# A written order for VectorE and GpSimd in a two-level Strassen feed-forward, on one core

## The chip, the cores and the metric

The kernel runs on one core of a Trainium2 chip. The metric is the device time in microseconds (us). Before the change it is 1205.03 us, the median of two runs (1204.66 and 1205.40). The profile is one further execution, with a span of 1208.1 us from its first to its last instruction.

## The reference

Batches of 576 tokens and 512 columns go through an attention whose key and query softmaxes are taken apart (so that keys times values comes first), then through a Fourier mixing layer, a layer norm and a feed-forward with residual:

```python
# B, H, S, DH = 8, 8, 576, 64;  D = 512;  FF = 2048
q_s = softmax(q, axis=-1);  k_s = softmax(k, axis=2)
x = q_s @ (k_s^T @ v)                    # per head; heads are put side by side: (8, 576, 512)
u = x + real(fft(fft(x, axis=1), axis=2))
un = (u - mean(u)) / sqrt(var(u) + 1e-6)
out = u + maximum(un @ w_ch1, 0) @ w_ch2  # w_ch1 (512, 2048), w_ch2 (2048, 512), all float32
```

## The kernel before

Tokens are taken in nine groups of 512 (own rows of eight batches, and one group of rows that all batches leave over). The program is written for a tile framework with a scheduler: the order of the source gives priorities, and the scheduler fixes, when the program is built, in which order each engine takes its instructions. Semaphores follow from the data.

The feed-forward of group 0 is plain. In groups in places 1 to 8 both matrix products are done with Strassen's seven products for a 2 x 2 split; the additions on the small side are made on the chip, those on the weights once and kept in DRAM. A product is numbered 1 to 7 and taken in `ORDER`; sums are made while PSUM is evicted:

```python
ORDER = (1, 6, 5, 7, 2, 4, 3)
# strassen(): one job = seven products into three PSUM banks ba, bb, bc
ends = {1: copy ba to s1 (ScalarE),
        6: u2 = bb + s1 (VectorE),
        7: u3 = bb + s1 (VectorE), out[2, 2](bc, u3),
        2: out[1, 1](ba), 4: out[2, 1](bb, s1), 3: out[1, 2](bc, u2)}
at = {1: "ba", 2: "ba", 6: "bb", 7: "bb", 4: "bb", 5: "bc", 3: "bc"}
```

The first layer (`up`, matmuls at L986) has four such jobs, called blocks here. `out` applies ReLU: for (1, 1) on ScalarE alone, for the others a VectorE addition (L997) and a ScalarE ReLU (L998). When a block is complete, GpSimd makes the four combinations of the hidden activations that the second layer's products need:

```python
def a_side(self, at, to, e1, e2):          # L377 to L380, both engines are GpSimd here
    e1.tensor_tensor(out=to(4), in0=at(2), in1=at(3), op=ALU.add)
    e1.tensor_tensor(out=to(2), in0=at(0), in1=at(2), op=ALU.subtract)
    e2.tensor_tensor(out=to(5), in0=to(4), in1=at(0), op=ALU.subtract)
    e2.tensor_tensor(out=to(6), in0=at(1), in1=to(5), op=ALU.subtract)
```

In the six groups in places 2 to 7 (`deep`), the second layer (`deep_down`, matmuls at L1091) is two-level: each of its seven products m is itself cut into seven sub-products n, 49 in all, of four 128x128 matmuls each. The products come in units that share banks. Before the sub-products of a unit, the same four additions are made on the quarters of its hidden activations (L1048), half on VectorE and half on GpSimd, while the unit before runs. Product 1 needs only the (1, 1) part of the first layer's result:

```python
UNITS = ((1,), (2, 4), (7, 6), (5, 3))
def a_steps(unit):
    for m in unit:
        to = own(m)
        for o, x, y, e, op in ((4, 2, 3, V, ALU.add), (2, 0, 2, V, ALU.subtract), (5, 4, 0, G, ALU.subtract),
                               (6, 1, 5, G, ALU.subtract)):
            steps.append(lambda ...: e.tensor_tensor(out=to(o), in0=to(x), in1=to(y), op=op))     # L1048
...
steps = a_steps(UNITS[0])
for i, unit in enumerate(UNITS):
    ahead = a_steps(UNITS[i + 1]) if i + 1 < len(UNITS) else []
    steps += mixed(unit_steps(unit), ahead) + after[unit]     # after: results added to x by GpSimd (L1054, L1057)
```

The weights of the second level are made in the group in place 1: `deepen` splits each of the seven combined parts of w2 into seven and stores them in DRAM.

Beside the feed-forward of a group runs the front of the next batch: the attention beside the first layer, the Fourier mix and the norm beside the second. The Fourier transform is folded by symmetry before its matmuls:

```python
def tokens_folded():   # L728: eo[i] = x[i % 2, 0] +- x[i % 2, 1], i < 2 on GpSimd, else VectorE
def columns_folded():  # L734: eo[i][1:256] +-= mirrored half, the same engines
def by_frequency():    # L743: sums of pairs of eo, i < 2 on GpSimd, else VectorE
def columns_again():   # L749, L750: eight VectorE additions on 128 columns
folds = [tokens_folded, columns_folded, by_frequency, folded]   # folded: columns_again, then the next keys' loads
return folds + [lambda: None] * (b > 1) + [lambda k=k: block(k) for k in (2, 3, 0, 1, 4)]
...
jobs, down = blk.up(order, unT), blk.down(g, order, unT)
merged(flat(jobs), one)                       # one: attention of the next batch
merged(down, two + norm(next group))          # two: folds, transform blocks, mixes
```

Of the kernel before, what the change touches and what calls it, by code (L numbers as in the profile page):

```python
# [40 lines left out]
F32 = mybir.dt.float32  # L41
# [37 lines left out]
UNITS = ((1,), (2, 4), (7, 6), (5, 3))  # L79
DEEP = [(m, n) for unit in UNITS for n in ORDER for m in unit]  # L80
PAIRS = [(j + NP // 2, j) for j in range(NP // 2)]
# [46 lines left out]
class _Block:  # L128
    def __init__(self, ctx, tc, q, kT, v, w1, w2, ft, cd, out):
# [46 lines left out]
        for at in range(1, B + 1):  # L176
            self.base[at] = len(self.plan)
            self.plan += [self.w1s[p][:].rearrange("p a n -> p (a n)") for pair in PAIRS for p in pair]
            if self.deep(at):
                for i in range(0, len(DEEP), 4):  # L180
                    self.plan.append(self.w2d[:, i:min(i + 4, len(DEEP)), :].rearrange("p a n -> p (a n)"))
            else:
                self.plan += [self.w2s[WB_AT[m]].rearrange("p a n -> p (a n)") for m in ORDER]
# [298 lines left out]

    def second_keys(self):
# [83 lines left out]
    def k_exp(self, it):  # L567
        nc, V = self.nc, self.nc.vector
        k = self.live[it][0]
        m = self.small.tile([P, 1], F32, tag="km", name="km", bufs=3)  # L570
        V.reduce_max(m[:], k, axis=AX.X, negate=True)
        rec = self.small.tile([P, 1], F32, tag="krec", name="krec", bufs=3)
        nc.scalar.activation(k, k, ACT.Exp, bias=m[:, 0:1], accum_out=rec[:, 0:1])
        V.tensor_scalar(out=rec[:], in0=rec[:], scalar1=ATT_EPS, scalar2=None, op0=ALU.add)
        V.reciprocal(rec[:], rec[:])
        self.live[it].append(rec)
# [15 lines left out]
    def k_times_v(self, it):  # L592
        nc, (_, b, r) = self.nc, it
        _, v, rec, ks = self.live.pop(it)
        pk = self.acc((P, P))
        for c in range(NC):
            nc.tensor.matmul(pk, lhsT=ks[:, c, :], rhs=v[:, c, :], start=(c == 0), stop=(c == NC - 1))  # L597
        for h in range(2):
            s = slice(64 * h, 64 * h + 64)
            to = self.kvr[b % 2][s, r, s]  # L600
            if b == 1:

                nc.scalar.mul(to, pk[s, s], rec[s, 0:1])
            else:
                nc.vector.tensor_scalar(out=to, in0=pk[s, s], scalar1=rec[s, 0:1], scalar2=None, op0=ALU.mult)
# [22 lines left out]
    def q_exp(self, it):  # L628
        nc, V = self.nc, self.nc.vector
        q = self.live[it][0]  # L630
        heads = q.rearrange("p (h d) -> p h d", h=H)
        spread = lambda t: t[:].unsqueeze(2).to_broadcast([P, H, DH])
        m = self.small.tile([P, H], F32, tag="qm", name="qm", bufs=3)
        V.reduce_max(m[:], heads, axis=AX.X, negate=True)  # L634
        for h in range(H):
            nc.scalar.activation(heads[:, h, :], heads[:, h, :], ACT.Exp, bias=m[:, h:h + 1])  # L636
        rec = self.small.tile([P, H], F32, tag="qrec", name="qrec", bufs=4)
# [3 lines left out]
        if it[:2] == ("q", 0) and it[2] == it[3]:  # L641


            self.live[it].append(spread(rec))
            return
# [21 lines left out]
    def t_fold(self, it):  # L667
# [4 lines left out]
        for e, op, i in ((G, ALU.add, 0), (V, ALU.subtract, 2)):  # L672
            e.tensor_tensor(out=T[:, :, i, 1:NT], in0=q[:, :, 1:NT], in1=q[:, :, W - 1:W - NT:-1], op=op)
            e.tensor_tensor(out=T[:, :, 1 + i, 1:NT - 1], in0=q[:, :, Q - 1:Q - NT + 1:-1],
                            in1=q[:, :, Q + 1:Q + NT - 1], op=op)
        n = NT - 1
# [5 lines left out]
    def q_times_kv(self, it):  # L682
# [3 lines left out]
        for r in range(NR):  # L686
            nc.tensor.matmul(px[:, r * P:(r + 1) * P], lhsT=qT[:, r, :], rhs=self.kvr[b % 2][:, r, :], start=True,  # L687
                             stop=True)
        x = self.xpart(b, c, u)
# [6 lines left out]
    def t_times_kv(self, b):  # L696
# [9 lines left out]
        nc.scalar.copy(self.xshared(b // 2)[part], px[W:])  # L706
        V.scalar_tensor_tensor(out=g[:, 1:HD], in0=g[:, D - 1:HD:-1], scalar=self.sign[:, 0:1], in1=g[:, 1:HD],
# [3 lines left out]
        self.live["g", b] = g  # L711
# [3 lines left out]
    def transform(self, b):  # L715
# [36 lines left out]
        def folded():  # L752
            columns_again()
# [39 lines left out]

        folds = [tokens_folded, columns_folded, by_frequency, folded] if b else [at_first]
# [140 lines left out]
    def strassen(self, product, out, early=lambda *a: None):  # L935
# [30 lines left out]
        for m in ORDER:  # L966
# [4 lines left out]
            steps.append(begin + parts + end)  # L971
        return steps

    def up(self, at, unT):
# [4 lines left out]
        for j in range(NP // 2):  # L979
# [24 lines left out]
            steps.append([s for m in job for s in m] + [lambda n=base + 2 * j + i: self.used(n) for i in range(2)])  # L1004
# [21 lines left out]
    def deep_down(self, g, at, unT):  # L1026

        nc, V, G = self.nc, self.nc.vector, self.nc.gpsimd
        base = self.base[at] + NP
        un = lambda i: unT[:, i].rearrange("p k n -> p (k n)").rearrange("p (f n) -> p f n", n=P)  # L1030
        dead = lambda m: [self.hblock(A_AT[m], a, b) for a, b in ((0, 1), (1, 0), (1, 1))]
        temps = {1: [self.gap(i) for i in range(3)], 4: [un(i) for i in range(3)], 2: [un(i) for i in range(3, 6)],
                 6: dead(1), 7: [self.gap(i) for i in range(3)], 5: dead(4), 3: dead(2)}
        result = {m: self.hblock(A_AT[m], 0, 0) for m in A_AT}
        tile = lambda m: result[m].rearrange("p (c e) n -> p c e n", c=2)

# [5 lines left out]
        def a_steps(unit):  # L1042
            steps = []
            for m in unit:
                to = own(m)
                for o, x, y, e, op in ((4, 2, 3, V, ALU.add), (2, 0, 2, V, ALU.subtract), (5, 4, 0, G, ALU.subtract),
                                       (6, 1, 5, G, ALU.subtract)):
                    steps.append(lambda to=to, o=o, x=x, y=y, e=e, op=op: e.tensor_tensor(out=to(o), in0=to(x), in1=to(y),  # L1048
                                                                                          op=op))
            return steps  # L1050
# [8 lines left out]
        def store(u):  # L1059
            for c in range(2):  # L1060
                self.store(g, c, u, self.xpart(g, c, u))

        after = {(1,): [lambda: into(0, 0, 1)],
                 (2, 4): [lambda: into(1, 0, 4), lambda: into(0, 0, 2)],
                 (7, 6): [lambda: sums(6, 1), lambda: into(0, 1, 6), lambda: sums(7, 6), lambda: into(1, 0, 7),
                          lambda: into(1, 1, 7)],
                 (5, 3): [lambda: into(1, 1, 5), lambda: store(1), lambda: into(0, 1, 5), lambda: into(0, 1, 3),
                          lambda: store(0)]}
        place = {1: "ba", 2: "ba", 6: "bb", 7: "bb", 4: "bb", 5: "bc", 3: "bc"}

        def unit_steps(unit):
            k, box = len(unit), {}

            def bank(n):
                box[n] = self.ps.tile([P, 2, P], F32, tag=n, name=n)

            def temp(n):
                box[n] = self.work.tile([P, 2, P], F32, tag=n, name=n, bufs=1)
                return box[n][:, 0:k]

            def product(n):
                def run(i):
                    m, to = unit[i], own(unit[i])
                    q = DEEP.index((m, n))
                    w = self.stream[base + q // 4]
                    first = n in (1, 6, 5)
                    if first and i == 0:
                        bank(place[n])
                    for f in range(4):
                        r = q % 4 * 4 + f  # L1090
                        nc.tensor.matmul(box[place[n]][:, i, :], lhsT=to(A_AT[n])[:, f, :],  # L1091
                                         rhs=w[:, r // 2, r % 2 * P:r % 2 * P + P], start=first and i == 0 and f == 0,
                                         stop=f == 3, skip_group_check=True)
                    if q % 4 == 3 or q == len(DEEP) - 1:
                        self.used(base + q // 4)
                return [lambda i=i: run(i) for i in range(k)]

            def plus(out, n, t):
                V.tensor_tensor(out=out, in0=box[n][:, 0:k], in1=t[:, 0:k], op=ALU.add)  # L1099

            def block(j, n, t=None):
                slots = [A_AT[m] for m in unit]
                out = self.hpairs(j)[:, slots[0]:slots[-1] + 1:max(slots[-1] - slots[0], 1), 0:P]
                if t is None:
                    nc.scalar.copy(out, box[n][:, 0:k])
                else:
                    plus(out, n, box[t])

            ends = {1: lambda: nc.scalar.copy(temp("s1"), box["ba"][:, 0:k]),  # L1109
                    6: lambda: plus(temp("u2"), "bb", box["s1"]),  # L1110
                    7: lambda: (plus(temp("u3"), "bb", box["s1"]), block(3, "bc", "u3")),
                    2: lambda: block(0, "ba"), 4: lambda: block(2, "bb", "s1"), 3: lambda: block(1, "bc", "u2")}
            steps = []
            for n in ORDER:
                steps += product(n) + ([ends[n]] if n in ends else [])
            return steps

        steps = a_steps(UNITS[0])
        for i, unit in enumerate(UNITS):
            ahead = a_steps(UNITS[i + 1]) if i + 1 < len(UNITS) else []  # L1120
            steps += mixed(unit_steps(unit), ahead) + after[unit]
        return steps

    def down(self, g, at, unT):
# [6 lines left out]
        def product(m, bank, first, final):  # L1131
# [6 lines left out]
            def run(i, q):  # L1138
                w = self.stream[n]
                if at == 1 and (i, q) == (order[0], 0):  # L1140
# [38 lines left out]
        return [s for m in steps for s in m]  # L1179
# [22 lines left out]
def kernel(ctx: ExitStack, tc: tile.TileContext, q, kT, v, w1, w2, ft,  # L1202
# [56 lines left out]

    groups = [*range(B - 1), B, B - 1]  # L1260
    for order, g in enumerate(groups):
        loads = [] if g == 0 else None
        one, two = front(order + 1, loads) if order + 1 < B else (blk.later, [])
# [46 lines left out]
        jobs, down = blk.up(order, unT), blk.down(g, order, unT)  # L1310

# [56 lines left out]
```

## Time and profile before

The spans are those of the profiled execution. TensorE is PE, its weight loads PEld, VectorE is DVE, ScalarE is ACT, GpSimd is POOL.

| what | value |
|---|---|
| device time | 1205.03 us |
| POOL idle before L377 of a block, waiting for ACT's ReLU | 251.5 us in 26 waits |
| PE matmuls of the first layer (L986), bank bb | 188.2 us, 768 records |
| PE matmuls of the second level (L1091), bank bb | 124.3 us, 912 records |
| additions L1048 on DVE | 76.0 us, 72 of them, 1075 ns each |
| additions L1048 on POOL | 91.7 us, 60 of them, 1537 ns each |
| DMA | 239.85 MB, mean 199 GB/s |

A timeline row gives start, length, engine, source line, operation, what it writes and reads, and how many instructions were merged; in brackets stands how long the engine was idle before it and what released it. A row of waits gives who waited for whom, the total in us, how often, and the longest. A row of busy time by stage gives the stretch, then for each engine its busy us and the number of instructions, and last the granted clock of TensorE (1.00 is full), the busy share of the DMA engines and GB/s. In the row of 40 slices each digit is the busy share in tenths.

### The profile page before, as it was taken

Reading aid. Unit: us, or ns where it says so; the run is one execution under the profiler, and the core shown is the slowest. Engines: PE = TensorE matmul, PEld = TensorE weight load, DVE = VectorE, ACT = ScalarE, POOL = GpSimd, SP = SyncE. Lnnn points to the kernel's source line nnn. Section 1 sums busy time; section 2 is a strip of 40 time slices with the busy share of each in tenths; the row PEclk is TensorE's granted clock in tenths of the full one; section 3 lists DMA queues with packets and bytes.
Section 4 is the critical chain, followed back from the end, with each engine's and each line's share of the span. In section 5 each row is a group of like instructions: output and inputs, shape, how many; then the busy total and the mean of one; then the engine's idle time right before and its main releaser. Section 6 shows DMA issues by size and latency. Waiting matters only on the chain.

```text
span 1208.1 us, 17183 instructions
## 1 busy us (share of the span) xinstructions
PE 1088.4 (90%) x6384; PEld 938.5 (78%) x6384; DVE 685.7 (57%) x1303; ACT 416.9 (35%) x1015; POOL 550.0 (46%) x449
## 2 busy tenths in 40 slices
PE   5799899988899699987999699969999799889998
PEld 4644457877788698877989698859988798789886
DVE  6784874477436884487445963586635743352211
ACT  6694424351216323361325232431334052101200
POOL 1075650355323654357333854276434834663420
PEclk9999999988999899998999899989999799989999
DMA  9475775576966356554565457635654456465541
GB/s 300 150 244 184 256 254 182 182 257 204 309 206 223 127 205 218 200 189 172 207 216 180 171 187 227 207 126 210 233 183 149 150 201 210 162 216 206 211 175 56
DMA packets 117507, 239.85 MB, mean 199 GB/s; under 512 B 24480, under 2 KB 77984, under 8 KB 106416
## 3 DMA queue, kind: packets, MB, share of 16 engines
q1 hardware_dynamic: 115624, 237.70, 57.1%
q10 hardware_dynamic: 1800, 1.05, 0.3%
q8 instruction: 51, 0.84, 0.3%
q14 instruction: 32, 0.26, 0.1%
HBM read 201.76 MB, written 41.16 MB: 201 GB/s over the span
## 4 chain that ended last, share of the span: by engine, by line
PE 66%; DVE 11%; POOL 7%; issue 2%; ACT 2%; DMA 1%; SPq 0%; POOLq 0%; DVEq 0%; ACTq 0%
PE bb L986 13%; PE bb L1091 9%; PE bc L986 8%; PE ba L986 8%; PE bc L1091 6%; PE ba L1091 5%; PE acc L597 2%; PE bc L1143 2%; PE acc L687 2%; DVE big L1048 2%; PE bb L1143 2%; POOL unT L1048 2%; PE bc L925 1%; POOL eo L728 1%; PE tr L886 1%
## 5 line engine op out<-in xcount | busy, mean ns | idle before, releaser
L986 PE MATMUL bb<-unT,big 128*128 128x256 f32 x768 | 188.2, 382 | 4.6 <-DVE unT L386 4.6
L1091 PE MATMUL bb<-big 128*128 128x128 f32 x912 | 124.3, 290 | 53.0 <-DVE big L1048 30.2
L986 PEld LDWEIGHTS bb<-unT,big 128*128 128x128 f32 x768 | 143.7, 191 | 26.2 <-DVE unT L386 7.4
L377 POOL TENSOR_TENSOR big<-big 128x512 f32<-128x512 f32 (+1 forms) x38 | 47.4, 1246 | 252.3 <-ACT big L998 251.5
L1091 PEld LDWEIGHTS bb<-big 128*128 128x128 f32 x912 | 116.4, 204 | 56.7 <-DVE big L1048 31.1
L998 ACT ACTIVATE big<-big 128x512 f32<-128x512 f32 x96 | 60.1, 629 | 211.2 <-DVE big L997 211.1
L986 PE MATMUL bc<-unT,big 128*128 128x256 f32 x512 | 125.6, 381 | 2.2 <-DVE unT L384 2.2
L986 PE MATMUL ba<-unT,big 128*128 128x256 f32 x512 | 122.7, 379 | 0.2 <-ACT unT L890 0.2
L1048 POOL TENSOR_TENSOR big<-big 128x512 f32<-128x512 f32 x60 | 91.7, 1537 | 38.0 <-DVE big L1048 34.2
L986 PEld LDWEIGHTS bc<-unT,big 128*128 128x128 f32 x512 | 95.3, 191 | 15.9 <-PE ba L986 4.0
L986 PEld LDWEIGHTS ba<-unT,big 128*128 128x128 f32 x512 | 95.3, 190 | 12.3 <-ACT unT L890 0.5
L1091 PE MATMUL ba<-big 128*128 128x128 f32 x672 | 90.4, 286 | 1.3 <-ACT s L1109 1.3
L1054 POOL TENSOR_TENSOR x<-x,big 128x512 f32<-128x512 f32 x45 | 65.4, 1469 | 55.8 <-DVE big L1099 39.7
L1091 PEld LDWEIGHTS ba<-big 128*128 128x128 f32 x672 | 86.2, 202 | 3.4 <-ACT s L1109 1.9
L1048 DVE TENSOR_TENSOR big<-big 128x512 f32<-128x512 f32 x72 | 76.0, 1075 | 13.8 <-POOL big L379 6.7
L958 DVE TENSOR_TENSOR u<-bb,s 128x512 f32<-128x512 f32 x34 | 23.5, 691 | 86.4 <-PE bb L986 65.7
L1091 PE MATMUL bc<-big 128*128 128x128 f32 x480 | 63.1, 284 | 7.0 <-DVE big L997 7.0
L1091 PEld LDWEIGHTS bc<-big 128*128 128x128 f32 x480 | 59.7, 200 | 7.5 <-DVE big L997 7.5
L636 ACT ACTIVATE q<-q,qm 128x64 f32<-128x64 f32 x240 | 61.7, 339 | 7.8 <-DVE qm L634 7.8
L997 DVE TENSOR_TENSOR big<-bc,u 128x512 f32<-128x512 f32 x64 | 44.1, 689 | 25.5 <-PE bc L986 24.1
L1099 DVE TENSOR_TENSOR u<-bb,s 128x256 f32<-128x256 f32 (+1 forms) x48 | 18.4, 384 | 69.2 <-PE bb L1091 68.8
L954 DVE TENSOR_TENSOR u<-bb,s 128x512 f32<-128x512 f32 x34 | 23.4, 690 | 58.6 <-PE bb L986 44.0
(276 smaller groups left out, 2112.0 us busy)
## 6 DMA issues: line engine op xcount, KB each, us to landing
big<-w2d SPq DMA_DIRECT2D x72, 1024.0 KB
big<-w1s SPq DMA_DIRECT2D x64, 896.0 KB
big<-w2s SPq DMA_DIRECT2D x14, 1024.0 KB
w2d<-big SPq DMA_DIRECT2D x49, 256.0 KB
big<-in_w_dram SPq DMA_DIRECT2D x21, 512.0 KB
q<-in_q_dram SPq DMA_DIRECT2D x27, 256.0 KB
k<-in_kT_dram SPq DMA_DIRECT2D x24, 288.0 KB
v<-in_v_dram SPq DMA_DIRECT2D x24, 256.0 KB
```

What stands on the lines that cost most here:

```text
L377: e1.tensor_tensor(out=to(4), in0=at(2), in1=at(3), op=ALU.add)
L597: nc.tensor.matmul(pk, lhsT=ks[:, c, :], rhs=v[:, c, :], start=(c == 0), stop=(c == NC - 1))
L636: nc.scalar.activation(heads[:, h, :], heads[:, h, :], ACT.Exp, bias=m[:, h:h + 1])
L687: nc.tensor.matmul(px[:, r * P:(r + 1) * P], lhsT=qT[:, r, :], rhs=self.kvr[b % 2][:, r, :], start=True, stop=True)
L958: V.tensor_tensor(out=temp("u3"), in0=box["bb"][:], in1=box["s1"][:], op=ALU.add)
L986: nc.tensor.matmul(bank()[:, i, :], lhsT=w[:, WA_AT[m], k * P:(k + 1) * P], rhs=unT[:, B_AT[m], k, :], start=first and i == 0 and k == 0, ...
L997: V.tensor_tensor(out=hp(i), in0=bank[:], in1=u[:], op=ALU.add)
L998: nc.scalar.activation(hp(i), hp(i), ACT.Relu)
L1048: steps.append(lambda to=to, o=o, x=x, y=y, e=e, op=op: e.tensor_tensor(out=to(o), in0=to(x), in1=to(y), op=op))
L1054: G.tensor_tensor(out=x, in0=x, in1=tile(m), op=ALU.add)
L1091: nc.tensor.matmul(box[place[n]][:, i, :], lhsT=to(A_AT[n])[:, f, :], rhs=w[:, r // 2, r % 2 * P:r % 2 * P + P], start=first and i == 0 an ...
L1143: nc.tensor.matmul(bank()[:, i, :], lhsT=h[p][:, A_AT[m], i * P:(i + 1) * P], rhs=w[:, p, :], start=first and i == 0 and p == 0, stop=p == ...
```

## The change

In the six deep groups the order in which VectorE and GpSimd take their instructions is no longer left to the scheduler. Every step of the group (feed-forward, the next batch's attention, transform and norm) gets a place on a time line; the steps are written out sorted by that place, and for these two engines the written order is kept (`manual_schedule`). TensorE and ScalarE are scheduled as before. The attention's steps are split so that an operation and the one that reads its far-off result have places of their own. With it come three changes of work: the folds of the transform are placed in the last part of the first layer; product 1 of the second layer is done one-level, so that it needs no additions; and of the four additions before each two-level product three are on VectorE and one on GpSimd. For two of the four query tiles of a batch the division by the softmax's sum is done where PSUM is evicted (for batches from the third on as well; before for the first only). The aim is that TensorE finds its next operands ready where the layers meet.

The core of the diff (cuts marked ...; what is moved only, or only split in two, is left out):

```diff
-UNITS = ((1,), (2, 4), (7, 6), (5, 3))
+UNITS = ((2, 4), (7, 6), (5, 3))
+DOWN_END = 8 + 3 * 2 * len(ORDER)
...
             if self.deep(at):
+                self.plan.append(self.w2s[WB_AT[1]].rearrange("p a n -> p (a n)"))
...
+    def attention_timed(self, b, end):
+        items = [("k", b, r) for r in range(NR)] + ([("t", b)] if b % 2 == 0 else [])
+        items += [("q", b, c, u) for c in range(2) for u in range(2)]
+        gap, steps = (end - 10) / (len(items) - 1), []
+        for i, it in enumerate(items):
+            t = i * gap
+            put(t - 2 * gap - 1, getattr(self, it[0] + "_load"), it)
+            if it[0] == "k":
+                for dt, f in ((0, self.k_max), (2, self.k_sum), (3, self.k_turn), (6, self.k_times_v), (7.7, self.k_scale)):
+                    put(t + dt, f, it)
+            elif it[0] == "q":
+                for dt, f in ((0, self.q_max), (5, self.q_sum), (6.5, self.q_turn), (9, self.q_times_kv), (10, self.q_out)):
+                    put(t + dt, f, it)
...
-        if it[:2] == ("q", 0) and it[2] == it[3]:
+        if it[0] == "q" and it[1] != 1 and it[2] == it[3]:      # the division waits for the eviction
...
+            folds = [(0, lambda: tokens_folded(two)), (0, lambda: tokens_folded(one)), (3, lambda: columns_folded(one)),
+                     (3, lambda: columns_folded(two)), (5, lambda: by_frequency(one)), (5.5, lambda: by_frequency(two)),
+                     (7, lambda: columns_again(one)), (11, folded)]
...
-        def a_steps(unit): ...
+        def a_step(m, o):
+            x, y, e, op = {4: (2, 3, V, ALU.add), 5: (4, 0, V, ALU.subtract), 2: (0, 2, V, ALU.subtract),
+                           6: (1, 5, G, ALU.subtract)}[o]
+            to = own(m)
+            e.tensor_tensor(out=to(o), in0=to(x), in1=to(y), op=op)
...
+        def single(i, q):                                        # product 1, one-level: 16 matmuls 128x256
+            for p in range(4 * q, 4 * q + 4):
+                nc.tensor.matmul(box["bb"][:, i, :], lhsT=h[p][:, A_AT[1], i * P:(i + 1) * P],
+                                 rhs=self.stream[base][:, p, :], start=i == 0 and p == 0, stop=p == NP - 1, ...)
...
+        for n in range(4):
+            put(2 * n, single, n // 2, n % 2)
+        n = 2 * len(ORDER)
         for i, unit in enumerate(UNITS):
+            t = 8 + n * i
+            for k, o in enumerate((4, 5, 2, 6)):
+                for j, m in enumerate(unit):
+                    put((0 if i == 0 else t - n + 2) + 3 * k + j * 1.2 + 0.3, a_step, m, o)
+            for k, o in enumerate(ORDER):
+                for j in range(2):
+                    put(t + 2 * k + j, product, unit, o, j)
+                put(t + 2 * k + 1.5, ends, unit, o)
...
-                if at == 1 and (i, q) == (order[0], 0):
+                if at == 1 and m != 1 and (i, q) == (order[0], 0):
                     self.deepen(...)
...
+    def timed_front(b):
+        end = 46
+        steps = blk.attention_timed(b, end)
+        dts = (0, 0, 3, 3, 5, 5.5, 7, 11)
+        steps += [(end + t, lambda i=i: make()[0][i][1]()) for i, t in enumerate(dts)]      # the folds
...
+        two = [((2, 4, 6, 8, 10)[k], lambda k=k: make()[1][k]()) for k in range(5)]         # transform blocks
+        return steps, two + [(13 + 4 * i, s) for i, s in enumerate(mixes)]
+    def timed_norm(g): ...                                       # places (26, 29, 31, 33, 35, 37, 40)
...
+        if timed:
+            end = 8 * len(ORDER)
+            steps = jobs + one + [(t + end, s) for t, s in down + two + timed_norm(groups[order + 1])]
+            rest = after_all
+            after_all = [(t - end - DOWN_END, s) for t, s in steps if t >= end + DOWN_END]
+            with tc.manual_schedule(engines={mybir.EngineType.DVE, mybir.EngineType.Pool}):
+                for _, s in sorted(rest + [s for s in steps if s[0] < end + DOWN_END], key=lambda s: s[0]):
+                    s()
+            continue
```

The first layer's four blocks take the places 0 to 56 (two steps of two matmuls for each product), the second layer the places 0 to 50 after that.

## The prediction

> **What bounds the kernel now.** I read the page's busy shares first, then TensorE's timeline end to end for its gaps, then the waits of TensorE, then a table of busy time by stage around one gap, and last VectorE and GpSimd inside that gap.
>
> ```profile
> PE 1088.4 (90%) x6384; PEld 938.5 (78%) x6384; DVE 685.7 (57%) x1303; ACT 416.9 (35%) x1015; POOL 550.0 (46%) x449
> PE   5799899988899699987999699969999799889998
> ```
>
> TensorE is busy 1088.4 of 1208.1 us; VectorE and GpSimd are at half. The slices show TensorE full but for the start and a dip that comes back once a group (the single 6s and 7s in the right two thirds). So the time is TensorE's work plus 119.7 us of gaps, and what matters is who makes the gaps. The waits of TensorE name VectorE:
>
> ```profile
> PE bb L1091 <- DVE big L1048: 30.2, 4, 8.7
> PE bb L1091 <- DVE u L1099: 21.1, 8, 7.6
> ```
>
> L1091 is the matmul of the two-level second layer, L1048 the additions on the hidden activations before a second-level product. In the timeline they look like this in the group whose second layer begins at 664.9 us (start, length, what, idle before it):
>
> ```profile
> 662.28 1.89 PE L986 MATMUL bc<-unT,big 128*128 128x256 f32 x8
> 664.00 1.05 PE L702 MATMUL acc<-kvr,F 128*128 128x128 f32 x8
> 664.89 1.06 PE L1091 MATMUL ba<-big 128*128 128x128 f32 x8
> 665.79 1.06 PE L1091 MATMUL bb<-big 128*128 128x128 f32 x8
> 667.99 1.16 PE L1091 MATMUL bc<-big 128*128 128x128 f32 x8 [1.14 <-DVE big L997]
> 670.02 1.16 PE L1091 MATMUL ba<-big 128*128 128x128 f32 x8 [0.87 <-ACT s L1109]
> 677.76 2.08 PE L1091 MATMUL bb<-big 128*128 128x128 f32 x8 [6.59 <-DVE big L1048]
> 679.63 2.66 PE L1091 MATMUL ba<-big 128*128 128x128 f32 x16
> 684.17 1.77 PE L1091 MATMUL bb<-big 128*128 128x128 f32 x8 [1.88 <-DVE u L1099]
> ```
>
> Idle here: 1.14 + 0.87 + 6.59 + 1.88 = 10.5 us. The same sum in the other two-level groups is 9.9, 12.2, 11.0, 8.9 and 8.8 us (second layers from 403.1, 533.9, 798.5, 930.4 and 1048 us): 61.2 us for the six. The first layer has almost none, and after the gap the second layer runs closed:
>
> ```profile
> core 0: us, PE busy (x) PEld busy (x) DVE busy (x) ACT busy (x) POOL busy (x), PEclk, DMA share, GB/s
> 601.80:664.90 63.10, 61.76 (x343) 54.98 (x342) 31.36 (x55) 25.91 (x63) 24.85 (x19) 1.00 0.60 204
> 664.90:682.00 17.10, 8.50 (x57) 7.93 (x56) 17.07 (x18) 3.80 (x10) 15.73 (x12) 0.80 0.34 133
> 682.00:733.40 51.40, 49.52 (x415) 48.78 (x414) 33.18 (x79) 15.20 (x39) 26.61 (x19) 0.97 0.56 201
> ```
>
> The reader should see that in the first 17 us of the second layer VectorE (17.07) is full and GpSimd nearly so (15.73), while in the 63 us before it they did 31 and 25. So the bound moves to VectorE and GpSimd for a quarter of each second layer. Why so much in 17 us: each L1048 addition is short alone and long beside GpSimd.
>
> ```profile
> 660.52 0.68 DVE L1048 TENSOR_TENSOR big<-big 128x512 f32<-128x512 f32 x1
> 673.02 1.75 DVE L1048 TENSOR_TENSOR big<-big 128x512 f32<-128x512 f32 x1
> 672.91 1.31 POOL L378 TENSOR_TENSOR big<-big 128x512 f32<-128x512 f32 x1
> ```
>
> Same shape, 0.68 against 1.75 us, with a GpSimd addition running. VectorE's additions out of PSUM kept 0.68 us in the same place (the two at L997).
>
> **What the Trainium skill says.** SBUF — State Buffer, section "SBUF: two separate sides": VectorE operations with two SBUF inputs and GpSimd operations that read SBUF take one shared pair of ports as an exclusive lock; the loser waits for the whole instruction. The lines just shown agree (0.68 becomes 1.75, about one GpSimd operation more). GPSIMD Engine Reference, section "4.1 Engine selection": GpSimd can't touch PSUM, so the evictions that TensorE waits for stay on VectorE; the trace has no GpSimd group with a PSUM operand. TensorE: Matmul & The Clock Gate, section "What's actually happening": an idle TensorE falls to half its clock and needs some 3.4 us of work to come back. It agrees: granted clock 0.80 in the 17 us window, and the 8 records after the gap take 1.87 us (677.76 to 679.63) against 0.90 (664.89 to 665.79).
>
> **The change, part by part.** The program has two trace records per f32 matmul: 4 blocks x 28 matmuls x 8 groups is 896, the first layer has 1792 records. A 128x256 record costs 1.72/8 = 0.215 us (662.28 to 664.00), a 128x128 one 0.90/8 = 0.112.
>
> 1. First product one-level. Removed: 7 sub-products x 4 matmuls x 2 = 56 records of 0.112, 6.3 us. Added: 16 matmuls x 2 = 32 records of 0.215, 6.9 us. TensorE pays 0.6 us more a group, six groups: +4 us. In exchange the additions for that product vanish (2 VectorE, 2 GpSimd). And the new product needs only the hidden quarter that ScalarE writes after the last block's product 2, with no addition at all, so TensorE has 6.9 us to do at the moment in which it stood.
>
> 2. Additions for the six other products: one more of the four goes to VectorE (3 + 1 in place of 2 + 2). VectorE 14 to 18 a group, GpSimd 14 to 6. GpSimd loses 8 x 1.53 us (the mean of L1048 there) = 12 us a group, and so the lock is asked for less.
>
> 3. The folds (token and column folds, by-frequency sums) of the next batch move into the last block of the first layer. In the 17 us window they were 2 x 1.44 + 2.35 + 1.15 us and more on VectorE, and 2.75 + 2.30 + 1.76 us on GpSimd. They leave the crowded window and go where VectorE is half used.
>
> Does it close the gap? In the compiled order of the changed kernel VectorE has, between the end of the first layer and the first second-level product that needs an addition (number 6), 2 evictions of 0.69, 4 additions of 0.7 to 1.75 us and some 1.3 us of small folds: 5.5 to 9.7 us. TensorE has the one-level product (6.9), the first sub-product of two m (1.8) and four blocks of the transform (0.99 each, as from 424.79 to 425.78 us): 12.7 us. So TensorE should not wait there. Gain: the 61.2 us of gaps, and the slow clock after them: 1.87 - 0.90 = 0.97 for the first 8 records and 2.66 - 1.95 = 0.71 for the next 16 (1.95 is what 16 take later in this stage), 1.7 us x 6 = 10 us.
>
> 4. The norm at a fixed place (40 steps of 50 into the second layer): its three VectorE additions on the normalised input stand before the last evictions, so the waits of 0.43 and 0.91 us at the start of five first layers (L986 on VectorE's unT) go: 6.7 us.
>
> 5. Group 1 no longer splits w2 for product 1: 2 + 2 additions and seven stores fewer. TensorE's gaps in that stage are 4.6 and 4.9 us, behind other things; I put 2 us.
>
> 6. Given back: VectorE takes its work in a written order, so an operation whose input is late holds what stands behind it. I looked for such places. In the last block of the first layer there stand between the evictions of product 6 and 7 one product with 1/sum (0.69), two token folds (1.48 each) and two column folds (1.2 each) beside GpSimd's own: 6 us, while TensorE has products 5, 7 and 2 before it needs that eviction, 5.2 us counting from 6. With the 0.7 of each eviction that is up to 2.3 us of wait. In the second layer a mix (2.6 us) and two additions (up to 3) stand before the eviction of product 7: about 1 us. I take 3 us a group, 18 us in all.
>
> Sum: -61 - 10 - 7 + 4 - 2 + 18 = -58, so 1205 - 58 = 1147 us.
>
> **Rivals.** (a) The order is wrong on the chip: VectorE stands still for ScalarE's exponentials or GpSimd and the evictions come late all through the first layer, which now has no gap. For it: the order was laid on a time line in which a step is two to four matmuls, and the first layer gets the folds on top of 31 to 38 us of VectorE. Against: VectorE would have some 42 of 63 us, and each reduction stands 1.7 to 4 us after what it waits for, while ten exponentials of a query tile took 2.49 us (at 655.91 us). If each of 24 blocks lost 2 us, the time would be about 1190. (b) Transfers become the limit: the second layer reads 11.5 MB in 57 instead of 68 us. For it: 407 GB/s in some slices. Against: the mean is 184 GB/s in that stage, no wait of TensorE names a transfer, and the first layer ran at 204 GB/s unhurt. It would cost 5 to 15 us: 1155. (c) The gap only moves: TensorE gets through the one-level product, then waits for product 6 or 7 since VectorE's 17 us of work is still there. For it: the window's VectorE was full, and 4 additions are moved to it. Against: item 3 takes about a third of that work out and item 1 another part. Half the gain would be left: 1175.
>
> **Range and chances.** With nothing given back and all gaps closed: 1205 - 61 - 10 - 7 + 4 - 2 = 1129, the best case. If 60% of it goes, rival (c) or part of (a), 1175. So 1128 to 1180 for 8 in 10. The 2% line is at 1181; only (a) in full or a blunder in the order reaches it. Faster 0.83, within 2% 0.10, slower 0.07.
>
> **What would show it.** TensorE idle at the start of each second layer under 2 us where it was 10; granted clock there near 1.0 and not 0.80; TensorE's busy total about 1082 (plus 4, minus 10); GpSimd's total down by some 70 us from 550; VectorE's contended additions shorter. Step 6 shows as waits of first-layer matmuls of bank bb for VectorE's u at L1032, one a group. The prediction is wrong if those waits come in every block, or if a TensorE wait for a transfer appears.

## The result, and the profile after

The changed kernel takes 1186.64 us (median of 1185.43 and 1187.85), 0.985 of the time before (95% interval 0.980 to 0.989): 18 us less, where 58 us less were predicted and the range ended at 1180. The profiled executions differ by 24.7 us in span (1208.1 and 1183.4), since that of before was 5 us above its median and that of after 1 us below; the lengths of stages below are read from them.

The page after, busy shares and slices of TensorE:

```profile
PE 1086.6 (92%) x6240; PEld 928.0 (78%) x6240; DVE 659.0 (56%) x1295; ACT 411.3 (35%) x997; POOL 478.1 (40%) x399
...
PE   5799899999798999799996999799987999999997
```

TensorE's gaps are 96.8 us where they were 119.7, and the dips in the slices have not gone: they stand at other places. The start of the second layer that was shown before (there 664.9 us, here 665.55) is now closed. The row of TensorE's timeline in which the one-level product (L1158) begins, and the table by stage of the same group:

```profile
665.55 3.72 PE L1158 MATMUL bb<-big 128*128 128x256 f32 x16 [0.40 <-DVE big L1071]
```

```profile
core 0: us, PE busy (x) PEld busy (x) DVE busy (x) ACT busy (x) POOL busy (x), PEclk, DMA share, GB/s
588.35:665.55 77.20, 65.13 (x342) 56.78 (x340) 39.87 (x75) 27.39 (x69) 25.79 (x21) 0.93 0.48 164
665.55:682.00 16.45, 16.42 (x101) 14.85 (x102) 10.42 (x19) 5.24 (x21) 10.51 (x7) 1.00 0.50 189
682.00:721.09 39.09, 38.63 (x346) 38.44 (x345) 26.16 (x57) 10.89 (x20) 18.56 (x13) 1.00 0.68 228
```

In the first 16.45 us of the second layer TensorE works 16.42 (8.50 of 17.1 before), VectorE 10.4 (17.1), and the granted clock is 1.00 (0.80). But the first layer, 63.1 us before, takes 77.2, at a clock of 0.93 and with 12 us of gaps (1.3 before). The waits of TensorE name who makes them:

```profile
PE tr L703 <- DVE q L697: 18.0, 3, 7.7
PE acc L765 <- POOL F L735: 13.4, 2, 6.7
...
PE acc L743 <- ACT qT L710: 8.3, 3, 4.2
...
PE bb L1060 <- DVE u L1032: 6.6, 5, 2.1
```

L703 are transposes of query tiles, L743 and L765 the products of queries and shared rows with keys-times-values: the attention of the next batch, not the feed-forward (L1060). In the timeline of this group's first layer:

```profile
618.48 1.89 PE L1060 MATMUL bc<-unT,big 128*128 128x256 f32 x8
...
621.53 1.10 PE L743 MATMUL acc<-kvr,qT 128*128 128x128 f32 x8
630.35 1.09 PE L703 MATMUL tr<-ident,q 128*128 128x128 f32 x4 [7.71 <-DVE q L697]
633.52 2.07 PE L743 MATMUL acc<-kvr,qT 128*128 128x128 f32 x8 [2.07 <-ACT qT L710]
635.38 1.91 PE L1060 MATMUL ba<-unT,big 128*128 128x256 f32 x4
```

TensorE has just finished block 2's last product; block 3's first stands behind two attention steps whose operand is not there. VectorE's timeline in the same stretch, and one row of GpSimd's:

```profile
624.36 1.12 DVE L776 SCALAR_TENSOR_TENSOR eo<-eo,sign 128x255 f32<-128x255 f32 x1 [0.94 <-ACT eo L768]
625.52 1.24 DVE L778 TENSOR_TENSOR eo<-eo 128x128 f32<-128x128 f32 x1
626.79 1.23 DVE L779 TENSOR_TENSOR eo<-eo 128x128 f32<-128x128 f32 x1
627.95 0.67 DVE L689 TENSOR_REDUCE qrec<-q 128x8 f32<-128x512 f32 x1
```

```profile
625.28 1.32 POOL L380 TENSOR_TENSOR big<-big 128x512 f32<-128x512 f32 x1
```

The sums of the second query tile (L689, and L697 after it) come last. In front of them in the written order stand three folds of the shared rows (L776 to L779), which nothing needs before the second layer. They wait for a ScalarE copy and then run beside GpSimd's four additions. That is the case of the two groups below called odd, 4 and 6, whose next batch is odd (so is that of group 2, where this wait is 2.6 us). In the two called even, 3 and 5, the operand is a GpSimd addition on shared rows (L735), written behind the four additions of a block. The last of the four, L735 and the matmul that waits, in group 3:

```profile
501.38 1.26 POOL L382 TENSOR_TENSOR big<-big 128x512 f32<-128x512 f32 x1
502.60 0.65 POOL L735 TENSOR_TENSOR F<-T 128x256 f32<-128x256 f32 x1
503.31 2.08 PE L765 MATMUL acc<-kvr,F 128*128 128x128 f32 x8 [6.69 <-POOL F L735]
```

By group, the lengths of the first and the second layer in us, from the first feed-forward matmul of each layer to that of the next in TensorE's timeline (groups are numbered by place; 2 to 7 are the deep ones, 7 has no next batch):

| kernel | layer | 2 | 3 | 4 | 5 | 6 | 7 | sum |
|---|---|---|---|---|---|---|---|---|
| before | first | 63.4 | 64.8 | 63.1 | 65.0 | 63.1 | 51.1 | 370.5 |
| before | second | 66.0 | 67.9 | 68.5 | 68.8 | 66.8 | 56.7 | 394.7 |
| after | first | 70.8 | 74.9 | 77.2 | 75.2 | 77.4 | 48.3 | 423.8 |
| after | second | 55.8 | 54.5 | 55.5 | 54.5 | 55.2 | 48.2 | 323.7 |

The second layers became 71.0 us shorter, the first ones 53.3 us longer. With the 7 us that went before group 2, this is the whole difference of the spans.

### The profile page after: what moved, and what is told of

It is laid out like the page before. It is cut to its first block, busy times and chain, and to the rows that moved or that the text cites. A ratio compares the mean times of both kernels' runs of the same rounds, so it can differ in the third digit from the quotient of the medians.

```text
span 1183.4 us, 16762 instructions
## 1 busy us (share of the span) xinstructions
PE 1086.6 (92%) x6240; PEld 928.0 (78%) x6240; DVE 659.0 (56%) x1295; ACT 411.3 (35%) x997; POOL 478.1 (40%) x399
## 5 line engine op out<-in xcount | busy, mean ns | idle before, releaser
L1060 PE MATMUL bb<-unT,big 128*128 128x256 f32 x768 | 189.1, 386 | 7.8 <-DVE u L1032 6.6
L379 POOL TENSOR_TENSOR big<-big 128x512 f32<-128x512 f32 (+1 forms) x38 | 46.4, 1222 | 326.7 <-ACT big L1072 325.9
L1060 PEld LDWEIGHTS bb<-unT,big 128*128 128x128 f32 x768 | 145.1, 193 | 31.9 <-DVE u L1032 9.5
L1060 PE MATMUL ba<-unT,big 128*128 128x256 f32 x512 | 128.1, 387 | 0.2 <-ACT unT L964 0.2
L1060 PE MATMUL bc<-unT,big 128*128 128x256 f32 x512 | 123.5, 380 | 0.2
L1060 PEld LDWEIGHTS ba<-unT,big 128*128 128x128 f32 x512 | 96.8, 195 | 12.5 <-ACT unT L964 0.5
L1060 PEld LDWEIGHTS bc<-unT,big 128*128 128x128 f32 x512 | 95.6, 191 | 12.7 <-DVE big L1071 0.6
L1177 PE MATMUL bb<-big 128*128 128x128 f32 x768 | 94.7, 275 | 1.0 <-DVE u L1184 1.0
L1177 PEld LDWEIGHTS bb<-big 128*128 128x128 f32 x768 | 90.1, 192 | 1.2 <-DVE u L1184 1.2
L1138 POOL TENSOR_TENSOR x<-x,big 128x512 f32<-128x512 f32 x45 | 59.4, 1333 | 56.0 <-ACT big L1163 20.8
L1177 PE MATMUL ba<-big 128*128 128x128 f32 x576 | 71.6, 276 | 2.8 <-ACT big L1198 2.8
L1134 DVE TENSOR_TENSOR big<-big 128x512 f32<-128x512 f32 x84 | 70.0, 864 | 7.2 <-POOL big L382 7.2
L1177 PEld LDWEIGHTS ba<-big 128*128 128x128 f32 x576 | 68.4, 192 | 5.1 <-ACT big L1198 3.9
L1134 POOL TENSOR_TENSOR big<-big 128x512 f32<-128x512 f32 x24 | 39.2, 1652 | 59.6 <-DVE big L1134 59.6
L1032 DVE TENSOR_TENSOR u<-bb,s 128x512 f32<-128x512 f32 x34 | 23.4, 689 | 70.7 <-PE bb L1060 48.3
L382 POOL TENSOR_TENSOR big<-big 128x512 f32<-128x512 f32 x32 | 48.8, 1526 | 2.3
L380 POOL TENSOR_TENSOR big<-big 128x512 f32<-128x512 f32 (+1 forms) x38 | 47.4, 1248 | 2.4
L743 PEld LDWEIGHTS acc<-kvr,qT 128*128 128x128 f32 x256 | 34.1, 204 | 17.6 <-ACT qT L710 13.8
```

The costliest lines, as they stand in the source:

```text
L1060: nc.tensor.matmul(bank()[:, i, :], lhsT=w[:, WA_AT[m], k * P:(k + 1) * P], rhs=unT[:, B_AT[m], k, :], start=first and i == 0 and k == 0, ...
L1138: G.tensor_tensor(out=x, in0=x, in1=tile(m), op=ALU.add)
L1177: nc.tensor.matmul(box[place[n]][:, i, :], lhsT=own(m)(A_AT[n])[:, f, :], rhs=w[:, r // 2, r % 2 * P:r % 2 * P + P], start=first and f == ...
```

## The experiments

Each is an edit of the changed kernel; "e3 and" means that e3's two edits are in it too. Ratios are to the kernel before.

**e1: the fold of shared rows later.**

```diff
-        put(t + 2, self.g_fold, b)
+        put(t + 8, self.g_fold, b)
```

> One number changed: the three small VectorE additions that fold the shared rows (g_fold) stand 8 places after the matmul they read instead of 2. Theory (place in the written order): in the two groups with an odd next batch they stand just before the row sums of the second query tile, 3.6 us of work beside GpSimd, and TensorE's next transpose waits for those sums; so its wait of 7.7 us falls to about 3 in both groups, nothing else moves, and the time falls by about 10 to 1177 us. Rival (VectorE and GpSimd have too much to do in the first layer): the wait comes back at the next operand, the time stays within 3 us of 1186.

Measured 1176.1 us, 0.977 (0.975 to 0.979). The wait of 7.7 us is 4.6 in both odd groups. Their first layers are 73.2 and 73.1 us (77.2 and 77.4); those of the even groups, which it should not touch, are 76.1 and 76.3 (74.9 and 75.2).

**e2: the shared query rows' second half earlier.**

```diff
-                put(t + 12, self.t_join)
+                put(t + 9.2, self.t_join)
```

> One number changed: the second half of the fold of the shared query rows (t_join, its GpSimd addition at L735) stands before the second block's four GpSimd additions instead of after them. Theory (place): TensorE's wait of 6.7 us for that addition in the two groups with an even next batch falls under 1.5 us, and with the slow clock after it the time falls by about 14 to 1172 us. Rival (too much work): GpSimd's four additions now come later by 0.6 us only, but the wait comes back elsewhere; the time stays within 3 us of 1186.

Measured 1173.0 us, 0.973 (0.972 to 0.975). The 6.7 us in both even groups are 0.6, their first layers are 67.0 us (74.9 and 75.2); those of the odd groups are 77.9 and 78.4 (77.2 and 77.4), with the same waits.

**e3: both edits.**

```diff
+                put(t + 9.2, self.t_join)
+        put(t + 8, self.g_fold, b)
```

> Both numbers changed. Theory (place): the gains add, as the waits are in different groups: about 1162 us (1186 - 10 - 14). Rival (too much work in the first layer): 1183 to 1189 us.

Measured 1159.3 us, 0.9625 (0.961 to 0.964). The gains add (10.5 + 13.6 against 27.4). Two numbers, no work changed, and more than the change itself had brought. Two rows of TensorE's waits in it (total, times, longest):

```profile
PE tr L703 <- DVE q L697: 11.3, 5, 4.6
...
PE acc L765 <- POOL F L735: 1.2, 2, 0.6
```

**e4: the scheduler's order again.**

```diff
-            with tc.manual_schedule(engines={mybir.EngineType.DVE, mybir.EngineType.Pool}):
+            with ExitStack():
```

> All changes of work are kept (one-level first product, folds in the first layer, three of four additions on VectorE, source sorted by place), but VectorE and GpSimd are ordered by the scheduler again. Theory (the work closed the gaps where the layers meet, the fixed order gave much of it back in the first layer): the second layer still starts without a gap over 3 us, the first layer's waits of 6.7 and 7.7 us are gone or small, about 1155 us. Rival (the fixed order itself closed the gaps): waits of 5 us and more stand again at the start of the second layer, 1190 to 1205 us.

Measured 1198.5 us, 0.9945 (0.9925 to 0.9966): the theory failed, and the time is in the rival's range. The long waits of the first layer are gone, but TensorE waits elsewhere: 3.0 to 3.1 us for the eviction of product 7 at each last block of groups 2 to 6, and in three groups 3.5 to 5.1 us for ScalarE's copy of the one-level product, 16 to 18 us into the second layer:

```profile
PE bb L1060 <- DVE u L1032: 16.0, 7, 3.1
...
PE bb L1177 <- ACT big L1163: 12.5, 3, 5.1
PE bb L1177 <- DVE u L1184: 11.8, 13, 1.9
```

Its second layers sum to 356.7 us, between before (394.7) and after (323.7), its first ones to 401.8. So the written order is worth about half of what the second layers gained. And the first layers are 31 us longer than before in the scheduler's order too: with the folds moved into them, not all of their loss is the written order's. (One wait in group 1, outside the groups in question, is 15.1 us long here and 6.8 in the changed kernel.)

**e5: TensorE's order written too.**

```diff
-            with tc.manual_schedule(engines={mybir.EngineType.DVE, mybir.EngineType.Pool}):
+            with tc.manual_schedule(engines={mybir.EngineType.DVE, mybir.EngineType.Pool, mybir.EngineType.PE}):
```

> The changed kernel with TensorE's order written too (same places), nothing else. Theory (the other half of each wait is TensorE's own order: the compiled order puts an attention matmul with a late operand ahead of first-layer matmuls that are ready): with half a product to a product and a half in front of it, the wait for the query sums in the two odd groups falls from 7.7 to about 3.5 us and the next one from 2.1 to 0.4, the one for the fold of shared rows in the even groups from 6.7 to about 5.8; about 1170 us. Rival (TensorE's order was good, only the operands were late): 1184 us or more.

Measured 1182.7 us, 0.981 (0.978 to 0.984): only 4 us under the changed kernel, between theory and rival. The waits themselves did as the theory said, more than it said in the even groups (7.7 to 3.46 in the odd, 6.7 to 3.35 in the even ones), so TensorE's own order is part of them. But the written order made new ones: 2.68 us for the norm in each of six second layers, 1.64 for a later query tile, and 58 to 59 us for second layers that took 55.

**e7: e3 and TensorE's written order.**

```diff
+            with tc.manual_schedule(engines={..., mybir.EngineType.PE}):
```

> Both places of e3 and TensorE's written order. Theory (two halves): what e3 left in the odd groups (4.6 us for the query sums, 0.7 us after, and the slow clock) goes, about 1147 us. Rival: within 3 us of e3's 1159, or above it because the written order of TensorE makes new waits.

Measured 1166.2 us, 0.968 (0.9655 to 0.970), 7 us above e3: the rival. First layers of the odd groups fall to 68.0, second layers rise to 56.6 to 59.4.

**e8: e3 and two more places.**

```diff
-                ... (9, self.q_times_kv), (10, self.q_out)):
+                ... (9, self.q_times_kv), (10 if it[2] else 12, self.q_out)):
-        dts = (0, 0, 3, 3, 5, 5.5, 7, 11)
+        dts = (0, 0, 3.6, 3, 5, 5.5, 7, 11)
```

> e3, and two more places: the product with 1/sum of the first query tile 2 places later (behind the second tile's sums), and the column folds of the transform just behind the eviction of product 7 of the last block instead of before it. Theory (place): TensorE's waits for that eviction (u at L1032; 1.8, 1.3, 1.2 us, 7.5 us in all) fall under 0.5 us each, the wait for the query sums falls by 0.7 us; about 1151 us. Rival: GpSimd's folds beside them are what makes VectorE late; within 3 us of 1159.

Measured 1163.8 us, 0.9655 (0.964 to 0.967), worse than e3. The waits at L1032 went, and came back one eviction later: 1.9 to 2.0 us before each one-level product, for product 4's bank. The wait for the query sums stayed at 4.6. That VectorE has more to do in the last block than fits between its evictions, so that an exchange inside it only moves the wait, is a reading of this; e14 fits it.

**e9: e3 with the folds in the second layer.**

```diff
-        dts = (0, 0, 3, 3, 5, 5.5, 7, 11)
+        dts = (11, 11, 14, 14, 16, 16.5, 18, 22)
-        two = [((2, 4, 6, 8, 10)[k], ...
+        two = [((13, 15, 17, 19, 21)[k], ...
-        return steps, two + [(13 + 4 * i, s) ...
+        return steps, two + [(23 + 4 * i, s) ...
-        ... enumerate((26, 29, 31, 33, 35, 37, 40))]
+        ... enumerate((33, 36, 38, 40, 42, 44, 47))]
```

> e3 with the folds of the transform put back into the second layer (11 places later, transform, mixes and norm 7 to 11 places later). Theory (the folds had to leave the crowded start of the second layer): TensorE waits for VectorE there or later in the second layer, 2 to 4 us a group, 1170 to 1180 us, though the waits for the last block's eviction go. Rival (the one-level product alone covers the start, and the place of the folds hardly matters): 1153 to 1162 us.

Measured 1209.3 us, 1.003 (1.002 to 1.005): 50 us above e3, far more than the theory's 11 to 21. The second layers are 67.3, 66.8, 67.0, 66.6 and 69.5 us, as long as before the change although product 1 is one-level (TensorE's gaps in these five are 40 us and not 52). Group 7, which has no folds, stays at 47.5. First e9 in group 3, then e3, each second layer whole:

```profile
529.18:595.93 66.75, 59.36 (x435) 56.78 (x434) 46.43 (x79) 15.81 (x39) 34.08 (x25) 0.92 0.54 181
```

```profile
522.67:577.15 54.48, 53.94 (x435) 52.18 (x435) 35.11 (x69) 15.78 (x40) 28.50 (x19) 1.00 0.65 222
```

The same instructions cost TensorE 5.4 us more (clock 0.92), and there are 6.9 us more of gaps. In e9 VectorE has no pause from 529.4 to 553.8 us in that layer's start, its folds standing among the additions (L1134), and TensorE waits for it there three times, 1.91, 1.98 and 1.08 us. (Two more stops come later, 0.46 us for ScalarE and 1.96 for VectorE.) The first two:

```profile
540.84 1.22 PE L1177 MATMUL bb<-big,unT 128*128 128x128 f32 x8 [1.91 <-DVE unT L1134]
...
547.39 0.51 PE L849 MATMUL acc<-ft,eo 128*128 128x144 f32 x2 [1.98 <-DVE eo L818]
```

The edit moves transform, mixes and norm with the folds, so their share is not apart, and it tries the folds at one set of places only.

**e10: e3 with the additions two and two.**

```diff
-                           5: (4, 0, V, ALU.subtract) ...
+                           5: (4, 0, G, ALU.subtract) ...
```

> e3 with the third of the four additions before each two-level product back on GpSimd (two and two, as before the change). Theory (GpSimd beside VectorE is what makes both slow at the start of the second layer): GpSimd has its four block combinations (4 x 1.6 us) and then two more additions before product 6 can run, 11 us after the start of the layer, while TensorE arrives there at about 12: at the edge, so 0 to 1 us a group, 1159 to 1166 us. Rival (the split did most of the gain): waits of 3 us and more at the start of each second layer, above 1177.

Measured 1158.2 us, 0.960 (0.958 to 0.963): no difference from e3. VectorE has 72 of the additions at L1134 where the changed kernel gives it 108. The largest group of them takes 1100 ns each instead of 864, and TensorE waits for one of all these additions once, 0.3 us. (The 72 and 60 additions in the table of the kernel before are also the largest groups; in all it had 84 on each engine.)

**e11: e3 with query maxima and sums earlier.**

```diff
-                for dt, f in ((0, self.q_max), (5, self.q_sum), ...
+                for dt, f in ((-1.5, self.q_max), (3.5, self.q_sum), ...
```

> e3 with the maxima and the sums of each query tile 1.5 places earlier. Theory (place): the second tile's sums come before the product with 1/sum of the first and before GpSimd's next four additions start, so the wait for the query sums in the two odd groups falls from 4.6 to about 2 us and the 0.7 after it goes; about 1152 us. Rival (the wait hangs on ScalarE's eight exponentials, which keep their place behind its other work): within 3 us of 1159.

Measured 1150.9 us, 0.954 (0.950 to 0.9575). First layers of the odd groups 69.9 and 70.2 (72.7 and 73.7). The wait for the sums is gone; the one for the ScalarE copy behind it, which should have gone too, grew from 0.7 to 2.6 us.

**e12: e3 with the attention ended at 43.**

```diff
-        end = 46
+        end = 43
```

> e3 with the whole attention squeezed so that it ends, and the folds begin, 3 places earlier (43 in place of 46). Theory (place): the folds no longer stand between the last block's evictions, the waits at L1032 (7.5 us in all) fall under 2, about 1153 us. Rival (a tighter attention makes other operands late): waits of the query transposes grow, 1160 to 1175.

Measured 1144.8 us, 0.9495 (0.947 to 0.952). The time came as expected and not for the reason given: the waits at L1032 stayed (1.7 us, five times), while the second query tile's transposes in the odd groups no longer wait 4.6 us for the sums (0.6 is left, for ScalarE's exponentials); their first layers fell to 66.9.

**e14: e3 with the attention ended at 40.**

```diff
-        end = 46
+        end = 40
```

> e12 with the folds 3 places earlier again (the attention ends at 40). In e12 the waits for the eviction of product 7 (L1032) stayed at 1.7 us a group, so the folds still stood between the evictions of products 6 and 7 of the last block; now they would stand before product 6. Theory (place): those waits fall under 0.7 us each, about 1138 us. Rival (the attention is squeezed too far): its operands come late again, 1146 us or more.

Measured 1133.6 us, 0.941 (0.939 to 0.943), 4.5% under the changed kernel and the best here. Now the waits at L1032 fall too. First layers sum to 372.3 us, as before the change (370.5) though the folds are in them; second layers to 322.2. Waits of TensorE, page and slices:

```profile
PE bb L1158 <- DVE big L1071: 4.5, 5, 1.1
...
PE bb L1060 <- DVE u L1032: 1.5, 5, 0.3
```

```profile
PE 1072.7 (95%) x6240; PEld 918.4 (81%) x6240; DVE 668.5 (59%) x1295; ACT 410.6 (36%) x997; POOL 475.5 (42%) x399
...
PE   5799989998979999999999999999999999999997
```

The slices are what the change was for: no dip in any deep group (these begin at 333 us; the 7 in slice 12, from 311 to 340 us, is a wait of group 1). VectorE even has a little more busy time than in the changed kernel (668.5 against 659.0).

## Why the prediction was wrong

**Where it held.** The gaps where the layers meet closed: the prediction has 61 + 10 - 4 = 67 us for them and the clock, and the second layers lost 71. TensorE waits at most 0.4 us there, at a clock of 1.00. But the changes of work in steps 1 to 3, to which the prediction gives this gain, brought 38 of the 71 us in the scheduler's order (e4); the rest came with the written order. GpSimd's total fell by 72 us (70 predicted). The waits of step 4 (L986 on unT) are not in the profile after. Group 7, which has no next batch and so none of step 6, lost 11.3 us; by the steps it should lose 8.8 + 1.7 + 1.3 - 0.6 = 11.2. The sum agrees better than its parts, which are 2.7 and 8.5 us for the two layers against 1.3 and 9.9. The wait that step 6 did work out, the eviction of product 7 in the last block, was sized "up to 2.3 us" and is 0.9 to 2.1.

**The step that failed is 6**, "I take 3 us a group, 18 us in all". The first layers gave back 53 us: 7.4, 10.1, 14.1, 10.2 and 14.3 in the five groups with a next batch, less the 2.7 that group 7 won. Of these, 38 us are gaps of TensorE (47.9 against 9.4), and 15 are the same matmuls taking longer. I had looked for late evictions only. The large waits are for operands of the attention: a fold that nobody needs soon, written before sums that TensorE needs at once (e1), and GpSimd's addition written after four others of 1.26 us each (e2). Two numbers took 27 of the 53 us back (e3), squeezing the attention by six places another 26 (e14), which ends 5 us above my best case of 1129. So the mechanism of the gain was right, and the term for what is given back was a third of its true size and stood in the wrong place.

Step 6 also puts the whole loss down to the written order. In the scheduler's order the first layers are still 31 us longer than before (e4), by other waits; in a written order with better places they are 2 us longer (e14). So it is the places that decide, and not the written order as such.

Rival (a) named about the right time, 1190, for another reason: evictions late in every block. They are not late, but for the last one. In groups 3 to 6 the gap is one or two long stops a group, and the long stops of 6.7 and 7.7 us go with a lower clock (0.93 to 0.95 in first layers that had 1.00). TensorE's own order is part of it: as compiled it has the attention's matmuls in front of ready first-layer matmuls. e5 shows that the stop shrinks when they stand further back, and that pinning TensorE as well costs more elsewhere. Why the scheduler put them there was not tried. Rivals (b) and (c) did not come: TensorE waits for a transfer once, 0.3 us, and never for the additions at L1134. The waits that cost the time were thus not among the signs of being wrong that the prediction named.

**Smaller points.** Step 2 (three additions on VectorE) was given weight as relief for the shared ports; in e3's kernel it is worth nothing in time (e10). Step 3 read its window wrongly: of the 6.4 us of VectorE's folds that it counts, 3.3 lie in 664.9 to 682.0, and they begin at 677.63, when the stop of 6.59 us ends (677.76). In groups 2, 3, 5 and 6 two token folds, 3.0 to 3.5 us, do come before the end of the stop. In the group shown VectorE had before it three folds of the shared rows (L707, L709, L710; 1.48, 1.15 and 1.34 us). The attention's new places take just these three into the first layer (L776 to L779 after), where step 6 does not count them and e1 finds them. Step 3 was not separated either. With the folds back in the second layer, at e9's places, the time is 50 us longer and the one-level product does not shorten the second layers of groups 2 to 6; whether folds further back in that layer, behind the additions, would cost as much was not tried. Where no folds are, in group 7, the layer goes from 56.7 to 50.2 us even in the scheduler's order (e4). Step 5 put 2 us on group 1's second layer; that layer is 0.8 us longer, while its first layer is 6.3 us shorter. Whether the division at the eviction, which reaches that batch too, does it was not tried.

## What to carry to other kernels

When the order of one engine is written by hand, list for each operation which engine stands still without it, and put first what another engine waits for next; work needed only in the next stage goes behind it, however early its input is there. The two longest kinds of stop here each came from wrong neighbours and shrank or went when one number was moved, so read the waits, look at what stood before the releaser on its engine, and move that. A move inside a stretch that is too full only moves the wait (e8); there work has to go to another stretch (e14). Keeping the folds out of the crowded seam between the layers was worth far more here (50 us at the places tried) than moving single additions from one engine to the other once it was empty (nothing).

## What was not expected of the hardware

Short stops can cost TensorE its clock too. The Trainium skill (TensorE: Matmul & The Clock Gate, section "What's actually happening") gives an idle window of about 3.4 us after which the clock is halved, and says that the window runs free. The measurement goes further: in group 3 of e9 the second layer's five stops are 0.5 to 2.0 us long, 7.4 us together, and yet the clock is 0.92 and the same matmuls take 5.4 us longer. Not every such stop costs it: the first layer of group 3 in e3 has stops of 0.6, 0.6 and 1.8 us and a clock of 1.00. In e8 16 records of the one-level product took 3.72 us after a stop of 2.00 (clock 1.00 from 522.5 to 526.5 us), and 5.41 after one of 1.91 (0.50 from 652 to 654 us). So the length of a stop alone does not decide; what does was not tried.

```profile
522.56 3.72 PE L1158 MATMUL bb<-big 128*128 128x256 f32 x16 [2.00 <-DVE big L1071]
```

```profile
650.61 5.41 PE L1158 MATMUL bb<-big 128*128 128x256 f32 x16 [1.91 <-DVE big L1071]
```

Small operations are hit hardest, in proportion, by GpSimd at work: in e9 a 128x128 addition at L817 took 0.28 us with GpSimd idle (at 550.38 us) and 1.35 beside it (at 544.71), nearly five times as long, where the 128x512 additions at L1048 went from 0.68 to 1.75. The one at L778 shown above took 1.24.
